# V in transfers of 4 MB and a stream of K and V in bursts, in a decode step of attention beside an MLP

## The chip, the cores and the metric

The kernel runs on one core of one Trainium2 chip. The metric is device microseconds of one execution. A timed run has no profiler; beside it stands one profiled execution, whose own time and span are given below.

## What is computed

One decode step (one new position) for a batch of 8, width D = 576. Two branches read the same x and are mixed by a gate:

```python
g = sigmoid((x * gate_w).sum(-1))            # one gate a batch
q = (x @ wq)                                  # 32 heads of 128
k, v = the last W = 2048 of 8192 positions    # 16 heads of K and V, each for two heads of q
o = softmax(q k^T / sqrt(128)) v              # for each batch and head
a = o @ wo                                    # 4096 -> 576
b = gelu(layernorm(x) @ w1 + b1) @ w2 + b2    # 576 -> 4608 -> 576
out = g * a + (1 - g) * b
```

All data are bfloat16. K and V within the window are 67 MB each, the weights some 20 MB; the rest is small.

## The kernel before, in words

**A plan, then five lists.** The kernel first describes all its work as operations with an engine, a cost and dependences (`_Plan`, lines 40 to 203). `schedule` walks through them in planned time, with a DMA rate of 428 GB/s and the costs given by hand, and so fixes the order of instructions on each engine; `emit` writes that order out, with semaphore waits where they are needed. At run time each engine goes through its own list in order. SyncE (SP) issues all large loads, in the order in which they are created, because each names the one before in `after`; a load that waits for its buffer holds back all loads behind it. ScalarE's queue issues the few small ones at the beginning (x, gate_w, b1).

**Buffers.** One arena in SBUF holds everything. Its largest part is `RAW`: nine slots of 2 MB (128 partitions of 16 KB). At the beginning wq lies in slots 0 to 2 and w1 in slots 3 to 5; slots 6 to 8 are empty. Hence line 642: slots 0 to 2 are free after the q projection (`o_qp`, lines 529 to 538, matmuls recorded at lines 411 and 413), slots 3 to 5 after the hidden layer's matmuls (`o_hp`, lines 560 to 571, the same two lines with other shapes).

**The beginning.** From x (line 451, sixteen rows: the batch twice) VectorE builds a spread and transposed x (lines 466 to 476), then the sums and the normalisation (477 to 491), gate and masks; then it transposes the projected q out of PSUM (line 541). ScalarE and TensorE turn that into query blocks (543 to 557). The hidden layer's five groups of matmuls come behind `o_qT` and behind the loads of w1 (line 570). The gate enters the second branch at line 494 (`dg`, for b2) and in `hs_fn` (598 to 601, for the hidden values).

**The stream.** Sixteen heads of K and V are taken in eight groups `g` of two heads; a group has four units `q` of K and four of V: head `2g + q // 2`, four batches, 2 MB. In a slot, a partition holds 64 positions of one batch in a row.
- `k_unit` (707 to 758) loads a K unit, VectorE transposes it in two halves (line 726, a STREAM_TRANSPOSE each), TensorE multiplies the query block with it (helpers at lines 405 and 420) into four PSUM banks that collect a whole group. After the fourth unit `softmax` follows: maximum on VectorE (672), exponentials on ScalarE (681), transposition of the weights (684). A K slot is free after its two transposes.
- `v_unit` (760 to 770) loads a V unit. When all four of a group have landed, `v_batch` multiplies (line 784, 64 matmuls a group), picks and folds the result (798 to 818) and scales it (`om_fn`, 822). V slots are free after the group's matmuls. The last group is done in two halves (`FULL`).
- `sums` and `rows` (687, 696) give the softmax's denominators for two groups; `wo_chunk` (832) loads a quarter of wo, forms rows by head and multiplies them into the result; its rows `oP` are cut at line 850.
- `bias` and `m2_chunk` (858, 866) load b2 and the four chunks of w2 at the end, the last in four pieces.

**The order of the loads** is `stream` (624 to 639): five K units ahead, then K and V in turn, a wo chunk after every eighth V unit, b2 and w2 at the end. `take_slot` (662) gives any of these the slot that an estimate (`slot_est`) says is free first. K, V, wo and w2 share all nine slots.

Of the kernel before, what the change touches and what calls it, by code (L numbers as in the profile page):

```python
# [8 lines left out]
ACTF = mybir.ActivationFunctionType  # L9
# [203 lines left out]
def build_kernel(nc, A_x, A_k_cache, A_v_cache, A_wq, A_wo, B_x, B_w1, B_b1, B_w2, B_b2, gate_w, out):  # L213
# [25 lines left out]
    with ExitStack() as es:  # L239
# [142 lines left out]
        def col(i, parts=128):  # L382
            return cols[0:parts, i:i + 1]
# [64 lines left out]
        o_qz = add("pool", lambda e: e.memset(view("qbd"), 0.0), name="qbd0", cost=1.0)  # L448


        d_x = dma("act", lambda e: e.dma_start(x_sb, bass.AP(x2.tensor, offset=x2.offset, ap=[[0, 2], [D, 8], [1, D]])), "x", 16 * D * 2, name="d_x")
        d_gw, d_gw1 = [dma("act", (lambda r0=r0, r1=r1: lambda e: e.dma_start(gw_sb[r0:r1, :], gate_w.partition_broadcast(r1 - r0)))(), "gw", (r1 - r0) * D * 2, name="d_gw%d" % r0, after=[d_x])
                       for r0, r1 in ((0, 6), (6, 8))]
        d_b1 = dma("act", lambda e: e.dma_start(b1c[0:FC, :], B_b1.rearrange("(c f) -> c f", c=FC)), "b", F * 2, deps=[o_pad], name="d_b1", after=[d_gw1])
        dx, dgw, db = [d_x], [d_gw, d_gw1], [d_b1]
        d_wqr = dma("sp", lambda e: e.dma_start(wq_r, A_wq[512:576, :].rearrange("k (s c) -> (k s) c", s=2)), "wq", 64 * 8192, name="d_wqr")
        d_wqm = dma("sp", lambda e: e.dma_start(wq_m.rearrange("p t c -> p (t c)"), A_wq[0:512, :].rearrange("(p t) c -> p (t c)", t=4)), "wq", 512 * 8192, name="d_wqm", after=[d_wqr])
        dwq = [d_wqm, d_wqr]
# [32 lines left out]
                                                               b1c[:, 32 * FJ * q:32 * FJ * (q + 1)].rearrange("p (i j) -> p j i", j=FJ)))(), deps=db, name="b1T%d" % q, cost=0.4, after=o_yT[-1:]) for q in range(4)]  # L491
        o_g = add("dve", lambda e: e.tensor_scalar(out=col(C_G), in0=col(C_T), scalar1=0.5, scalar2=0.5, op0=ALU.mult, op1=ALU.add), deps=[o_t] + o_tq, name="g", cost=0.12)
        o_omg = add("dve", lambda e: e.tensor_scalar(out=col(C_OMG), in0=col(C_T), scalar1=-0.5, scalar2=0.5, op0=ALU.mult, op1=ALU.add), deps=[o_t] + o_tq, name="omg", cost=0.12)
        o_dgb = add("dve", lambda e: e.tensor_scalar(out=dg, in0=idf8, scalar1=col(C_OMG, 8), scalar2=None, op0=ALU.mult), deps=[o_omg, o_idf], name="dgb", cost=0.12)

        def gb_fn(e):
            src = bass.AP(arena_f, offset=foffs("cols") + C_G, ap=[[AST // 2, 128], [1, 2], [0, 32]])
# [98 lines left out]
        o_hf = add("dve", lambda e: e.scalar_tensor_tensor(out=v1_sb, in0=v2_sb, scalar=1.0, in1=uh_sb, op0=ALU.add, op1=ALU.mult), deps=[o_th, o_uh], name="hf", cost=0.4)  # L596

        def hs_fn(e):
            in1 = bass.AP(arena_f, offset=foffs("gb") + 32, ap=[[AST // 2, 128], [0, FT], [1, 8]])
            return e.tensor_tensor(out=hT, in0=v1_sb.rearrange("p (t b) -> p t b", b=8), in1=in1, op=ALU.mult)  # L600
        o_hT = add("dve", hs_fn, deps=[o_hf, o_gb], name="hT", cost=0.4)


# [17 lines left out]


        NUQ = 4 * NG
        stream = [("K", i) for i in range(5)]
        ki, vi = 5, 0
        while ki < NUQ or vi < NUQ:
            if ki < NUQ:
                stream.append(("K", ki))
                ki += 1
            if vi % 8 == 3:  # L630
                stream.append(("R", vi // 4))
            if ki >= 6:
                stream.append(("V", vi))
                if (vi + 1) % (NUQ // (Hq // WO_CH)) == 0:
                    stream.append(("W", vi // (NUQ // (Hq // WO_CH))))
                vi += 1
                if vi % 8 == 3:
                    stream.append(("S", vi // 4))
        stream += [("B", 0)] + [("M", i) for i in range(FC)]

        last_dma = [d_w1r]
# [9 lines left out]
        sel_done, oP_ev, rc_last, sum_pe = [], [], [], {}  # L651

        def src_of(cache, g, q):
            hkv, b0 = 2 * g + q // 2, 4 * (q % 2)
            return cache[b0:b0 + 4, hkv, S0:Sk, :].rearrange("a (x r) d -> x a (r d)", x=32)

        FULL = 7
        slot_est = [18.0 + s for s in range(3)] + [38.0 + s for s in range(3)] + [s - 9.0 for s in range(3)]
        landed = [22.0]
        UT, WT = 4 * W * Dh * 2 / P.DMA_BW, WO_CH * 128 * D * 2 / P.DMA_BW  # L660

        def take_slot(took, hold):
            landed[0] += took
            s = min(range(NSLOT), key=lambda s: slot_est[s])
            assert slot_free[s] is not None
            slot_est[s] = landed[0] + hold
            return s

        def softmax(g):
# [36 lines left out]

        def k_unit(i):
            g, q = divmod(i, 4)
            s = take_slot(UT, 8.0)
            d = dma("sp", lambda e: e.dma_start(slot(s), src_of(A_k_cache, g, q)), "s%d" % s, 4 * W * Dh * 2, deps=slot_free[s], name="dk%d" % i, after=last_dma[-1:])  # L710
            last_dma.append(d)
            ub = q
            qrs = []
            if q == 0:
                def qr_fn(e):
                    dst = bass.AP(arena, offset=aoffs("qbd"), ap=[[AST, 128], [128, 16], [32, 4], [1, 8]])
                    in0 = bass.AP(arena, offset=aoffs("q4") + 128 * g, ap=[[AST, 128], [8, 16], [0, 4], [1, 8]])
                    in1 = bass.AP(arena_f, offset=foffs("mq"), ap=[[AST // 2, 128], [0, 16], [1, 4], [0, 8]])
                    return e.tensor_tensor(out=dst, in0=in0, in1=in1, op=ALU.mult)  # L719
                qrs.append(add("pool", qr_fn, deps=[o_q4, o_qz, o_mq, qk_unit.get(i - 1)], name="qr%d" % g, cost=0.8))  # L720
            trs = []
            for h in range(2):
                n = 2 * i + h
                kb = n % 2
                deps = [d] + ([qk_half[n - 2]] if n >= 2 else [o_ssq])
                tr = add("dve", (lambda h=h, kb=kb: lambda e: e.transpose(bass.AP(arena_f, offset=foffs("KT") + kb * 2048, ap=[[AST // 2, 128], [1, 2048]]),  # L726
                                                                         bass.AP(arena_f, offset=foffs("RAW") + s * (SE // 2) + 32 * h, ap=[[AST // 2, 128], [64, 64], [1, 32]])))(),
                         deps=deps, name="tr%d_%d" % (i, h), cost=2.3, after=tr_hist[-1:])
                tr_hist.append(tr)
                trs.append(tr)  # L730

                first = q == 0 and h == 0

                def qk_fn(e, h=h, kb=kb, first=first):
                    mm = None
                    if first:
                        mm_row(e, maskL, [ps[:, rc, :] for rc in range(2)], [maskR] * 2, True, False)
                        late_wait()
                        for rc in range(2, 4):
                            held_mm(e, ps[:, rc, :], maskL, maskR, True, False)  # L740
# [12 lines left out]
                qk = add("pe", qk_fn, deps=deps, late=late, name="qk%d_%d" % (i, h), cost=1.95 + (0.9 if first else 0), after=qk_half[-1:])  # L753
                qk_half.append(qk)
            qk_unit[i] = qk
            slot_free[s] = trs
            if q == 3:
                softmax(g)

        def v_unit(i):  # L760
            g, q = divmod(i, 4)
            full = g < FULL
            s = take_slot(UT, (3 - q if full else q == 0) * 2 * UT + (10.0 if full else 5.0))
            d = dma("sp", lambda e: e.dma_start(slot(s), src_of(A_v_cache, g, q)), "s%d" % s, 4 * W * Dh * 2, deps=slot_free[s], name="dv%d" % i, after=last_dma[-1:])
            last_dma.append(d)
            v_wait.append((q, s, d))
            slot_free[s] = None
            if q == 3 or not full and q >= 1:
                v_batch(g, list(v_wait))
                v_wait.clear()  # L770
# [59 lines left out]
                oT_done[it] = om  # L830

        def wo_chunk(i):
            s = take_slot(WT, 14.0)
            h0 = WO_CH * i
            dst = slot(s)[:, 0:WO_CH * D]
            d = dma("sp", lambda e: e.dma_start(dst, A_wo[128 * h0:128 * (h0 + WO_CH), :].rearrange("(p t) c -> p (t c)", t=WO_CH)),
# [4 lines left out]
            def rows_fn(e):  # L841
                mm = None
                for h in range(WO_CH):
                    mm = e.matmul(ps[:, bk, 64:64 + 8 * WO_CH], wide[:, 112 - 16 * h:240 - 16 * h], oX[:, i % 2, h, :], start=(h == 0), stop=(h == WO_CH - 1), skip_group_check=True)
                    if h == 0:
# [1 line left out]
                return mm  # L847
            its = range(h0 // 2, (h0 + WO_CH) // 2)
            sel_done.append(add("pe", rows_fn, deps=[oT_done[it] for it in its] + [o_wide, rc_last[-1]] + oP_ev[-1:], late=[[d]], name="orow%d" % i, cost=0.6))
            oP_ev.append(add("act", lambda e: e.activation(out=oP[:, i % 2, :], in_=ps[:, bk, 64:64 + 8 * WO_CH], func=ACTF.Copy),  # L850
                             deps=[sel_done[-1]] + ([proj_ops[i - 2]] if i >= 2 else []), name="oPev%d" % i, cost=0.25, prio=3))
            mms = [(oP[:, i % 2, 8 * t:8 * t + 8], dst[:, t * D:(t + 1) * D]) for t in range(WO_CH)]
            proj_ops[i] = AccGroup("proj%d" % i, mms, [oP_ev[-1], d], cost=0.25 * WO_CH).op
# [10 lines left out]
            o_m2.append(AccGroup("m2_b", [(ob[:, 0:8], b2_sb), (ob[:, 8:16], b2_sb)], ds + [o_obl, o_obh], cost=0.6).op)  # L864

        def m2_chunk(ci):
            s = take_slot(FCW * D * 2 / P.DMA_BW, 6.0)
            dst = slot(s)[:, 0:FJ * D]
            src = B_w2[FCW * ci:FCW * ci + FCW, :].rearrange("(p j) n -> p (j n)", j=FJ)
            cuts = [0, 4, 7, 8, 9] if ci == FC - 1 else [0, FJ]  # L870
# [94 lines left out]
```

## Time and profile before

| What | Value |
|---|---|
| timed runs | median 367.14 us (366.82 to 367.57, 3 runs) |
| the profiled execution, whole | 368.24 us |
| its span, first to last instruction | 366.5 us |
| bytes by DMA | 154.50 MB, mean 422 GB/s |
| TensorE / VectorE busy | 229.9 / 229.5 us (63% each) |
| ScalarE / GpSimd busy | 23.4 / 23.1 us |
| granted TensorE clock, mean | 0.823 |

The page shows one execution. Shares are of the span; a line such as L726 is line 726 of the kernel. A helper's line (405, 411, 413, 420, 616) stands for all who call it. The rows of slices cut the span into 40 equal parts of 9.2 us. "PEld" is TensorE's loading of weights. Times in the span begin at its first instruction.

### The profile page before, as it was taken

Reading aid. Unit: us, or ns where it says so; the run is one execution under the profiler, and the core shown is the slowest. Engines: PE = TensorE matmul, PEld = TensorE weight load, DVE = VectorE, ACT = ScalarE, POOL = GpSimd, SP = SyncE. Lnnn points to the kernel's source line nnn. Section 1 sums busy time; section 2 is a strip of 40 time slices with the busy share of each in tenths; the row PEclk is TensorE's granted clock in tenths of the full one; section 3 lists DMA queues with packets and bytes.
Section 4 is the critical chain, followed back from the end, with each engine's and each line's share of the span. In section 5 each row is a group of like instructions: output and inputs, shape, how many; then the busy total and the mean of one; then the engine's idle time right before and its main releaser. Section 6 shows DMA issues by size and latency. Waiting matters only on the chain.

```text
span 366.5 us, 2720 instructions
## 1 busy us (share of the span) xinstructions
PE 229.9 (63%) x1356; PEld 42.4 (12%) x892; DVE 229.5 (63%) x256; ACT 23.4 (6%) x36; POOL 23.1 (6%) x38
## 2 busy tenths in 40 slices
PE   0319883973956768753965396554965395574674
PEld 0000000000200011100200022000300021002232
DVE  1994899787854586447964655459744765456210
ACT  1001002002000020002000200002000200002000
POOL 8001001001000100001000100000000100000100
PEclk9977997897886669866888889887986689768659
DMA  8999999999999999999999999999999999999994
GB/s 343 429 412 438 426 427 433 431 433 431 431 426 431 427 437 429 431 431 429 431 429 429 427 437 431 427 431 433 429 427 433 432 431 431 431 429 429 424 428 186
DMA packets 11462, 154.50 MB, mean 422 GB/s; under 512 B 1294, under 2 KB 1590, under 8 KB 2106
## 3 DMA queue, kind: packets, MB, share of 16 engines
q1 hardware_dynamic: 11392, 154.29, 98.6%
q8 instruction: 9, 0.15, 0.1%
q10 hardware_dynamic: 58, 0.05, 0.0%
q14 instruction: 3, 0.02, 0.0%
HBM read 154.32 MB, written 0.01 MB: 421 GB/s over the span
## 4 chain that ended last, share of the span: by engine, by line
DMA 47%; DVE 25%; PE 23%; ACT 2%; issue 2%; SPq 1%; DVEq 0%
DMA arena<-in_A_k_cache_dram 40%; PE ps L405 11%; DVE arena L726 10%; DMA arena<-in_B_w_dram 5%; PE ps L420 4%; DVE arena L672 4%; PE ps L784 4%; DVE arena L684 2%; ACT arena L681 2%; DMA arena<-in_A_x_dram 2%; PE ps L413 2%; DVE arena L679 1%; DVE arena L471 1%; PE ps L411 1%; DVE arena L675 1%
## 5 line engine op out<-in xcount | busy, mean ns | idle before, releaser
L726 DVE STREAM_TRANSPOSE arena<-arena 128x2048 f32<-128x2048 f32 x64 | 145.2, 2294 | 72.0 <-DMA arena<-in_A_k_cache_dram 68.9
L405 PE MATMUL ps<-arena 128*128 128x512 bf16 x408 | 141.5, 463 | 0.0
L420 PE MATMUL ps<-arena 128*128 128x512 bf16 x136 | 64.6, 475 | 94.7 <-DVE arena L726 54.1
L420 PEld LDWEIGHTS ps<-arena 128*128 128x128 bf16 x136 | 15.4, 113 | 226.4 <-DVE arena L726 101.4
L784 PE MATMUL ps<-arena 128*32 128x512 bf16 x512 | 33.2, 404 | 2.7 <-DMA arena<-in_A_v_cache_dram 2.7
L672 DVE TENSOR_REDUCE arena<-ps 128x1 f32<-128x2048 f32 x8 | 18.3, 2287 | 25.1 <-PE ps L405 25.1
L681 ACT ACTIVATE arena<-ps,arena 128x2048 bf16<-128x2048 f32 x8 | 15.7, 1967 | 183.4 <-DVE arena L679 183.4
L684 DVE STREAM_TRANSPOSE arena<-arena 128x2048 bf16<-128x2048 bf16 x8 | 18.2, 2275 | 2.1 <-ACT arena L681 2.1
L719 POOL TENSOR_TENSOR arena<-arena 128x512 bf16<-128x512 bf16 x8 | 8.3, 1038 | 170.0 <-PE ps L405 156.6
L411 PE MATMUL ps<-arena 128*32 128x512 bf16 (+2 forms) x40 | 7.3, 708 | 15.4 <-DMA arena<-in_A_wq_dram 15.4
L784 PEld LDWEIGHTS ps<-arena 128*32 128x32 bf16 x512 | 12.6, 100 | 26.7 <-issue 13.0
L827 POOL TENSOR_TENSOR arena<-arena 128x256 bf16<-128x256 f32 (+1 forms) x9 | 6.0, 666 | 153.2 <-ACT arena L818 153.2
L616 PE MATMUL ps<-arena 128*8 128x288 bf16 (+1 forms) x140 | 11.6, 315 | 3.6 <-DMA arena<-in_B_w_dram 2.3
L413 PE MATMUL ps<-arena 128*32 128x384 bf16 (+2 forms) x56 | 9.9, 760 | 0.0
L801 DVE COPY_PREDICATED arena<-arena,ps 128x128 f32<-128x128 int32 x30 | 9.0, 300 | 1.0
L800 DVE COPY arena<-ps 128x128 f32<-128x128 f32 x10 | 2.7, 275 | 10.1 <-PE ps L784 10.0
L809 PE MATMUL ps<-arena 128*128 128x32 f32 (+2 forms) x20 | 4.4, 298 | 6.8 <-DVE arena L801 6.8
L891 DVE CAST arena<-ps 8x288 bf16<-8x288 f32 x1 | 0.4, 446 | 12.4 <-PE ps L616 12.4
L818 ACT ACTIVATE arena<-ps 128x32 f32<-128x32 f32 (+1 forms) x9 | 2.0, 221 | 96.1 <-PE ps L809 96.1
L471 DVE TENSOR_SCALAR arena<-arena 16x64 bf16<-16x64 bf16 (+1 forms) x6 | 4.0, 798 | 5.1 <-DMA arena<-in_A_x_dram 5.0
L616 PEld LDWEIGHTS ps<-arena 128*8 128x8 bf16 (+1 forms) x140 | 6.0, 92 | 8.0 <-DMA arena<-in_B_w_dram 3.7
L549 PE MATMUL ps<-arena 128*128 128x256 bf16 x4 | 1.1, 405 | 7.7 <-ACT arena L543 7.7
(78 smaller groups left out, 63.6 us busy)
## 6 DMA issues: line engine op xcount, KB each, us to landing
arena<-in_A_k_cache_dram SPq DMA_DIRECT2D x32, 2048.0 KB, 30.0
arena<-in_A_v_cache_dram SPq DMA_DIRECT2D x32, 2048.0 KB, 29.5
arena<-in_B_w_dram SPq DMA_DIRECT2D x1, 4608.0 KB, 24.3
arena<-in_A_wo_dram SPq DMA_DIRECT2D x4, 1152.0 KB, 29.6
arena<-in_A_wq_dram SPq DMA_DIRECT2D x1, 4096.0 KB, 14.1
arena<-in_B_w_dram SPq DMA_DIRECT2D x3, 1296.0 KB, 17.4
arena<-in_B_w_dram SPq DMA_DIRECT2D x2, 576.0 KB, 21.3
arena<-in_A_wq_dram SPq DMA_DIRECT2D x1, 512.0 KB, 3.4
```

The costliest lines, as they stand in the source:

```text
L405: return e.add_instruction(mybir.InstMatmult(name=nc.get_next_instruction_name(), ins=[e.lower_ap(rhs), e.lower_ap(lhsT)], outs=[e.lower_a ...
L411: mm = e.matmul(outs[0], lhsT, rhss[0], start=start, stop=stop, skip_group_check=True, tile_position=pos)
L413: mm = e.add_instruction(mybir.InstMatmult(name=nc.get_next_instruction_name(), ins=[e.lower_ap(r), e.lower_ap(lhsT)], outs=[e.lower_ap(o) ...
L420: mm = e.matmul(outs[0], lhsT, rhss[0], start=start, stop=stop)
L616: ins = e.matmul(ps[32 * j:32 * j + 8, BK_ACC, 0:JN], lhsT, rhs[:, JN * j:JN * j + JN], start=first and i == 0, stop=True, skip_group_chec ...
L672: mx = add("dve", lambda e: e.tensor_reduce(out=k(MX), in_=ps[:, 0:4, :].rearrange("p a n -> p (a n)"), axis=AXL.X, op=ALU.max), deps=[qk_ ...
L681: ex = add("act", lambda e: e.activation(out=Pm, in_=ps[:, 0:4, :].rearrange("p a n -> p (a n)"), func=ACTF.Exp, bias=k(NB), scale=SCALE, ...
L684: pt_done[g] = add("dve", lambda e: e.transpose(bass.AP(arena, offset=aoffs("PT") + (g % 2) * 2048, ap=[[AST, 128], [8, 64], [512, 4], [1, ...
L719: return e.tensor_tensor(out=dst, in0=in0, in1=in1, op=ALU.mult)
L726: tr = add("dve", (lambda h=h, kb=kb: lambda e: e.transpose(bass.AP(arena_f, offset=foffs("KT") + kb * 2048, ap=[[AST // 2, 128], [1, 2048]]),
L784: mm = e.matmul(ps[32 * t:32 * t + 32, bank, :], PT[:, g % 2, q, 32 * r4:32 * r4 + 32], slot(s)[:, 512 * r4:512 * r4 + 512], start=j < 4, ...
L801: return e.copy_predicated(buf, bass.AP(arena_i, offset=foffs("m4") + r, ap=[[AST // 2, 128], [0, 128]]), src)
```

## The change

Three things go together.

**One V transfer for all eight batches.** A V head's two units are now loaded by one DMA of 4 MB into two neighbouring slots: a partition takes 64 positions of two batches that follow each other, 32 KB, and so the first slot holds the even batches, the second the odd ones. To match, K units take every second batch instead of four in a row. The batch order inside the kernel thereby is 0, 2, 4, 6, 1, 3, 5, 7: x is loaded in that order by two DMAs of eight rows each, and the places where the order meets the outer one (the b2 rows, the hidden values, `oP`) write with a changed pattern. The last group's V is still loaded in units of 2 MB.

**Bursts.** Eight K units come first; then, for each group, its V, (after every second one) a wo chunk, and the K of the group after the next.

**Slots.** V of the first seven groups always uses slots 0 to 3. K, wo and the last V go round slots 6, 7, 8, 4, 5. The four w2 chunks use slots 0 to 3.

```diff
-        d_x = dma("act", lambda e: e.dma_start(x_sb, bass.AP(x2.tensor, offset=x2.offset, ap=[[0, 2], [D, 8], [1, D]])), "x", 16 * D * 2, name="d_x")
+        d_x0, d_x = [dma("act", (lambda s: lambda e: e.dma_start(x_sb[8 * s:8 * s + 8, :], bass.AP(x2.tensor, offset=x2.offset, ap=[[D, 2], [2 * D, 4], [1, D]])))(s), "x", 8 * D * 2, name="d_x%d" % s)
+                     for s in range(2)]
...
-        dx, dgw, db = [d_x], [d_gw, d_gw1], [d_b1]
+        dx, dgw, db = [d_x0, d_x], [d_gw, d_gw1], [d_b1]
...
-        stream = [("K", i) for i in range(5)]
-        ki, vi = 5, 0
-        while ki < NUQ or vi < NUQ:
...
+        stream = [("K", i) for i in range(8)]
+        for g in range(NG):
+            if g % 2 == 0:
+                stream += [("S", g), ("R", g)]
+            stream += [("V", 4 * g + q) for q in range(4)]
+            if g % 2:
+                stream.append(("W", g // 2))
+            if g + 2 < NG:
+                stream += [("K", 4 * (g + 2) + q) for q in range(4)]
         stream += [("B", 0)] + [("M", i) for i in range(FC)]
...
-            hkv, b0 = 2 * g + q // 2, 4 * (q % 2)
-            return cache[b0:b0 + 4, hkv, S0:Sk, :].rearrange("a (x r) d -> x a (r d)", x=32)
+            return cache[q % 2:B:2, 2 * g + q // 2, S0:Sk, :].rearrange("a (x r) d -> x a (r d)", x=32)
...
-        def take_slot(took, hold):
-            landed[0] += took
-            s = min(range(NSLOT), key=lambda s: slot_est[s])
...
+        ring = [6, 7, 8, 4, 5]
+
+        def take_slot():
+            s = ring.pop(0)
+            ring.append(s)
             return s
...
-            s = take_slot(UT, (3 - q if full else q == 0) * 2 * UT + (10.0 if full else 5.0))
-            d = dma("sp", lambda e: e.dma_start(slot(s), src_of(A_v_cache, g, q)), "s%d" % s, 4 * W * Dh * 2, deps=slot_free[s], name="dv%d" % i, after=last_dma[-1:])
-            last_dma.append(d)
+            s = q if full else take_slot()
+            if not full:
+                d = dma("sp", lambda e: e.dma_start(slot(s), src_of(A_v_cache, g, q)), "s%d" % s, 4 * W * Dh * 2, deps=slot_free[s], name="dv%d" % i, after=last_dma[-1:])
+                last_dma.append(d)
+            elif q % 2:
+                src = A_v_cache[0:B, 2 * g + q // 2, S0:Sk, :].rearrange("a (x r) d -> x a (r d)", x=32)
+                d = dma("sp", lambda e: e.dma_start(RAW[:, (q - 1) * SE:(q + 1) * SE], src), "s%d" % (q - 1), 8 * W * Dh * 2, deps=slot_free[q - 1] + slot_free[q], name="dv%d" % i, after=last_dma[-1:])
+                last_dma.append(d)
+            else:
+                d = None
...
         def m2_chunk(ci):
-            s = take_slot(FCW * D * 2 / P.DMA_BW, 6.0)
+            s = ci
```

Left out: the four patterns that put the batches back in order (`dg`, `hT`, `oP` and their sources), each one instruction as before.

More of the change, by code (lines that the diff above doesn't have):

```diff
@@ L493, in build_kernel @@
         o_omg = add("dve", lambda e: e.tensor_scalar(out=col(C_OMG), in0=col(C_T), scalar1=-0.5, scalar2=0.5, op0=ALU.mult, op1=ALU.add), deps=[o_t] + o_tq, name="omg", cost=0.12)
-        o_dgb = add("dve", lambda e: e.tensor_scalar(out=dg, in0=idf8, scalar1=col(C_OMG, 8), scalar2=None, op0=ALU.mult), deps=[o_omg, o_idf], name="dgb", cost=0.12)
+        o_dgb = add("dve", lambda e: e.tensor_scalar(out=dg.rearrange("p (b s) -> p s b", s=2), in0=idf8.rearrange("p (s b) -> p s b", s=2), scalar1=col(C_OMG, 8), scalar2=None, op0=ALU.mult), deps=[o_omg, o_idf], name="dgb", cost=0.12)
         def gb_fn(e):
@@ L598, in hs_fn @@
         def hs_fn(e):
-            in1 = bass.AP(arena_f, offset=foffs("gb") + 32, ap=[[AST // 2, 128], [0, FT], [1, 8]])
-            return e.tensor_tensor(out=hT, in0=v1_sb.rearrange("p (t b) -> p t b", b=8), in1=in1, op=ALU.mult)
+            in1 = bass.AP(arena_f, offset=foffs("gb") + 32, ap=[[AST // 2, 128], [0, FT], [4, 2], [1, 4]])
+            return e.tensor_tensor(out=hT.rearrange("p t (b s) -> p t s b", s=2), in0=v1_sb.rearrange("p (t s b) -> p t s b", s=2, b=4), in1=in1, op=ALU.mult)
         o_hT = add("dve", hs_fn, deps=[o_hf, o_gb], name="hT", cost=0.4)
@@ L623, in build_kernel @@
         NUQ = 4 * NG
-        stream = [("K", i) for i in range(5)]
-        ki, vi = 5, 0
-        while ki < NUQ or vi < NUQ:
[L627 to L638, printed above, removed]
+        stream = [("K", i) for i in range(8)]
[7 more added lines that the diff above has]
+                stream += [("K", 4 * (g + 2) + q) for q in range(4)]
         stream += [("B", 0)] + [("M", i) for i in range(FC)]
@@ L653, in src_of @@
         def src_of(cache, g, q):
-            hkv, b0 = 2 * g + q // 2, 4 * (q % 2)
-            return cache[b0:b0 + 4, hkv, S0:Sk, :].rearrange("a (x r) d -> x a (r d)", x=32)
+            return cache[q % 2:B:2, 2 * g + q // 2, S0:Sk, :].rearrange("a (x r) d -> x a (r d)", x=32)
         FULL = 7
-        slot_est = [18.0 + s for s in range(3)] + [38.0 + s for s in range(3)] + [s - 9.0 for s in range(3)]
-        landed = [22.0]
-        UT, WT = 4 * W * Dh * 2 / P.DMA_BW, WO_CH * 128 * D * 2 / P.DMA_BW
-        def take_slot(took, hold):
-            landed[0] += took
-            s = min(range(NSLOT), key=lambda s: slot_est[s])
-            assert slot_free[s] is not None
-            slot_est[s] = landed[0] + hold
+        ring = [6, 7, 8, 4, 5]
+        def take_slot():
+            s = ring.pop(0)
+            ring.append(s)
             return s
@@ L708, in k_unit @@
             g, q = divmod(i, 4)
-            s = take_slot(UT, 8.0)
+            s = take_slot()
             d = dma("sp", lambda e: e.dma_start(slot(s), src_of(A_k_cache, g, q)), "s%d" % s, 4 * W * Dh * 2, deps=slot_free[s], name="dk%d" % i, after=last_dma[-1:])
@@ L762, in v_unit @@
             full = g < FULL
-            s = take_slot(UT, (3 - q if full else q == 0) * 2 * UT + (10.0 if full else 5.0))
-            d = dma("sp", lambda e: e.dma_start(slot(s), src_of(A_v_cache, g, q)), "s%d" % s, 4 * W * Dh * 2, deps=slot_free[s], name="dv%d" % i, after=last_dma[-1:])
-            last_dma.append(d)
+            s = q if full else take_slot()
[8 more added lines that the diff above has]
+                d = None
             v_wait.append((q, s, d))
-            slot_free[s] = None
             if q == 3 or not full and q >= 1:
@@ L832, in wo_chunk @@
         def wo_chunk(i):
-            s = take_slot(WT, 14.0)
+            s = take_slot()
             h0 = WO_CH * i
@@ L849, in wo_chunk @@
             sel_done.append(add("pe", rows_fn, deps=[oT_done[it] for it in its] + [o_wide, rc_last[-1]] + oP_ev[-1:], late=[[d]], name="orow%d" % i, cost=0.6))
-            oP_ev.append(add("act", lambda e: e.activation(out=oP[:, i % 2, :], in_=ps[:, bk, 64:64 + 8 * WO_CH], func=ACTF.Copy),
+            oP_ev.append(add("act", lambda e: e.activation(out=oP[:, i % 2, :].rearrange("p (t b s) -> p t s b", b=4, s=2), in_=ps[:, bk, 64:64 + 8 * WO_CH].rearrange("p (t s b) -> p t s b", s=2, b=4), func=ACTF.Copy),
                              deps=[sel_done[-1]] + ([proj_ops[i - 2]] if i >= 2 else []), name="oPev%d" % i, cost=0.25, prio=3))
```

## The prediction

> **What bounds the kernel now.** I read the head of the profile's page first, then the DMA queues, then stretches of the span.
>
> ```profile
> span 366.5 us, 2720 instructions
> ...
> GB/s 343 429 412 438 426 427 433 431 433 431 431 426 431 427 437 429 431 431 429 431 429 429 427 437 431 427 431 433 429 427 433 432 431 431 431 429 429 424 428 186
> ...
> q1 hardware_dynamic: 11392, 154.29, 98.6%
> ...
> DMA 47%; DVE 25%; PE 23%; ACT 2%; issue 2%; SPq 1%; DVEq 0%
> ...
> L726 DVE STREAM_TRANSPOSE arena<-arena 128x2048 f32<-128x2048 f32 x64 | 145.2, 2294 | 72.0 <-DMA arena<-in_A_k_cache_dram 68.9
> ...
> L784 PE MATMUL ps<-arena 128*32 128x512 bf16 x512 | 33.2, 404 | 2.7 <-DMA arena<-in_A_v_cache_dram 2.7
> ```
>
> The chain gives DMA only 47%, but it follows one dependence after another. The better view is SP's queue q1: its packets keep the 16 DMA engines busy for 98.6% of the span, and no slice between the first and the last falls below 412 GB/s. A stretch of 40 us, the busiest for VectorE, shows the same from another side (the columns are the stretch, its length, the busy time of TensorE, its weight loads, VectorE, ScalarE and GpSimd, then clock, DMA share and GB/s):
>
> ```profile
> 46.00:86.00 40.00, 27.95 (x108) 2.60 (x26) 34.33 (x25) 2.06 (x2) 2.08 (x2) 0.91 1.01 430
> ```
>
> The queue is never empty, and at 430 GB/s the 154.29 MB alone take 358.8 us of the 366.5. VectorE, the busiest engine beside it, has 34.3 us of work in these 40. So the change can win only by a higher rate or by the few microseconds at the two ends, and it loses whatever time it lets the queue run empty.
>
> The end has a little air in it:
>
> ```profile
> 360.00:361.00 1.00, 0.36 (x6) 0.28 (x8) 0.00 (x0) 0.00 (x0) 0.00 (x0) 1.00 0.89 347
> 361.00:362.00 1.00, 0.91 (x16) 0.46 (x10) 0.00 (x0) 0.00 (x0) 0.00 (x0) 1.00 0.56 203
> 362.00:363.00 1.00, 0.66 (x8) 0.27 (x8) 0.00 (x0) 0.00 (x0) 0.00 (x0) 1.00 0.08 30
> 363.00:364.00 1.00, 0.70 (x10) 0.30 (x10) 0.00 (x0) 0.00 (x0) 0.00 (x0) 1.00 0.09 28
> ```
>
> The shares add up to 1.62 engine-microseconds per engine after 360: the mean DMA engine is done at about 361.6, and the last at about 363.9. From 362 on, 0.08 of 16 is little more than one engine. One engine lags the mean by some 2.3 us and all but it are done by about 362.3. A hole that most engines see costs nothing until it is larger than their 1.6 us of lead.
>
> **The change part by part.** *The bytes* stay: 28 V blocks of 2 MB become 14 transfers of 4 MB, K stays at 2 MB. I price the 14 saved transfer boundaries at 0. With 2 MB transfers, the stretch already runs at 430 GB/s and a DMA share of 1.01, so a boundary hides no time that a share could show. Bounds: 438 GB/s is the best slice of the page; V's 58.7 MB at 438 in place of 430 would be 58.7/430 - 58.7/438 = 2.5 us faster. At 412, the worst slice, it would be 6.0 us slower.
>
> The Trainium skill, page "DMA: Bandwidth & Descriptors", section "Anatomy of one DMA", gives a DMA about 2 us of fixed cost; by that, 14 fewer would save 28 us. The trace does not agree for transfers queued back to back (share 1.01), so that sum is not used.
>
> *The stream in its steady part.* A K block of 2.097 MB takes 4.88 us at 430 GB/s, a burst of four 19.5 us, a V group as long. Two transposes of a K block take VectorE 2 x 2.29 = 4.59 us, so it keeps pace with a burst; the softmax falls into the V half. With five slots in turn, the fifth block after a K block needs that block transposed: the wait falls on a block of the burst before, which is read some 20 us earlier. V's next 4 MB needs the 64 matmuls of the group before; 512 take 33.2 us, so 64 take 4.2, twice that at half clock. Against 8 us stand four K blocks, 19.5 us, already in the queue. Cost 0, margin about 11 us; SP waits there, with the next K blocks behind it, and that delays nothing until the margin is gone. The weights of the output projection pass through the K ring once in two groups and need their slot back 40 us later: 0.
>
> *The end* keeps its order (V of the last head pair in single blocks, output weights, bias, four chunks of B_w2). The chunks get V's four slots, which are free earlier than now; the queue is full there in both: 0. The regrouped batch rows (gate, hidden, oP) change patterns of instructions that exist already: 0, at most tenths of a microsecond off the path.
>
> *The beginning* is where I find a price. The fourth K block now gets slot 4, which held w1 and is free only after the hidden layer's matmuls (line 413). Before, the fourth to sixth K blocks took slots that the query weights had left:
>
> ```profile
> 0.79 0.39 SPq L456 DMA_DIRECT2D arena<-in_A_wq_dram  x1
> ...
> 2.77 18.45 SPq L710 DMA_DIRECT2D arena<-in_A_k_cache_dram  x6
> 37.10 0.53 SPq L764 DMA_DIRECT2D arena<-in_A_v_cache_dram  x1
> 37.85 0.54 SPq L710 DMA_DIRECT2D arena<-in_A_k_cache_dram  x1
> ```
>
> Six blocks were issued by 21.2. The row at 37.85 is the first use of a w1 slot, and SP's wait before it is the end of line 413. In the changed order that is K block 3, and only three blocks (0 to 2) cover the time until then. How long do they last?
>
> ```profile
> 0.00:40.10 40.10, 16.96 (x111) 2.09 (x47) 26.02 (x56) 2.82 (x4) 9.81 (x22) 0.87 0.96 406
> ```
> ```profile
> L710 SPq DMA_DIRECT2D arena<-in_A_k_cache_dram x2: 615/887/1159, 3.5 to 4.7; - x2
> ...
> DMA to landing us min/median/max: 33.9/35.7/37.6
> ```
> ```profile
> 0.00:1.80 1.80, 0.00 (x0) 0.00 (x0) 0.00 (x0) 0.00 (x0) 1.20 (x5) 1.00 0.00 0
> 1.80:2.10 0.30, 0.00 (x0) 0.00 (x0) 0.00 (x0) 0.00 (x0) 0.30 (x2) 1.00 1.32 259
> ```
>
> wq, w1 and three blocks are 4.72 + 5.31 + 6.29 = 16.32 MB, with x 16.35; 406 GB/s x 40.1 us = 16.28 MB, so the mean engine is through with block 2 at 40.2. The next two rows are those of K issues 1 and 2 (at 3.5 and 4.7; shortest, median and longest time to landing): block 2 lands at 4.7 + 37.6 = 42.3, less some 0.3 from data to landing 42.0 for the slowest engine. The first issue, at 0.79, moved its first byte at 1.8: 1.0 us. Block 3 would move from 37.85 + 1.0 = 38.9, 1.3 us before the mean engine runs dry and 3.1 before the slowest does. So the hole is (delay of line 413) - 1.3 us for the mean engine.
>
> Line 413 will be later, since it hangs on x:
>
> ```profile
> 0.79 7.14 DMA arena<-in_A_x_dram
> 8.03 2.07 DVE arena L471 x3
> ...
> 25.45 1.17 DVE arena L541
> ...
> 27.08 1.14 PE ps L549 x4
> ...
> 37.09 0.74 PE ps L413 x6
> ```
>
> From x's landing at 7.93 VectorE works without a pause to the transpose of q (line 541), then ScalarE, the selection matmuls, the hidden layer. A delay d of x goes through in full. Its small DMAs share the engines with wq rows of 32 KB, each 32768 B / (430/16 GB/s) = 1.22 us. These are the packets of ACT's queue in the windows 0 to 4.3, 4.3 to 6.2 and 6.2 to 8.03:
>
> ```profile
> q10 hardware_dynamic: 14, 0.02, 1.3%
> ```
> ```profile
> q10 hardware_dynamic: 5, 0.00, 0.7%
> ```
> ```profile
> q10 hardware_dynamic: 8, 0.00, 0.7%
> ```
> ```profile
> 0.79 1.22 ACTq L451 DMA_DIRECT2D arena<-in_A_x_dram  x1
> 2.04 0.66 ACTq L452 DMA_DIRECT2D arena<-in_gate_w_dram  x2
> ```
>
> Fourteen went before the big rows were under way, then about one per 1.22 us and engine: from 4.3 to 7.93 are three turns, the last rows of x and its completion. Now x comes in two DMAs; the second is issued at 2.04 instead of with the first. It misses the quick start, and its eight rows, on few engines as x's three turns suggest, take four turns and one for the completion. Starting at 5.3 to 6.2 (the turn after a wait like that of the first, about 2.9 us from the issue) it lands at 10.5 to 11.4: d = 2.6 to 3.5. Bounds: 0, if both halves fit into the quick start, and 6, two turns more. I take 3.4, for ACT's second issue stood at 2.04 and its packets show only past 4.3. The hole: 3.4 - 1.3 = 2.1 us for the mean engine, 0.3 for the slowest. At the end the others have 1.6 us of lead, so +0.5 us (2.1 - 1.6; the laggard itself gives 0.3).
>
> The Trainium skill, page "DMA: Bandwidth & Descriptors", section "Queues, rings and completion order", has each DMA engine go round-robin between its queues packet by packet; this agrees with the turns of 1.22 us.
>
> **Sum.** Against the profiled execution: 366.5 + 0.5 = 367.0 us of span. That execution took 368.24 in all; the median of the three timed runs is 367.14. I add the +0.5 to the median: **367.6 us**. About 0.2% (0.73 us) is what a measurement of this kernel can tell from no change.
>
> **The rivals.** *Cover holds* (x's halves both make the quick start, d under 1.3): no hole, 367.1. For it: 14 small packets passed by 4.3. Against it: the second issue comes 1.25 us later.
>
> *A longer hole, slower.* Place: before K block 3. From d = 3.7 on (mean hole 2.4) it passes 0.73 us at the end and then costs one for one. With one or two turns more, d = 4.6 to 5.9, the mean hole is 3.3 to 4.6: +1.7 to +3.0; I take +2.0, 369.1. A slow-clock stretch over line 413 would act alike.
>
> *A better rate.* V at 435 GB/s in place of 430: 58.7/430 - 58.7/435 = 1.6 us, 365.5. For it: slices of 437 and 438. Against it: whole stretches of 40 us stay at 430.
>
> *V's slots starve the queue.* With PV's end 11 us later than I reckon, each of seven groups loses what goes beyond; 1 us each is +7, 374.
>
> *Strided batches.* K blocks now take every second batch, 67 MB apart in place of 33.5 (16 heads x 8192 x 128 x 2 B a batch). If that brought K's 67.1 MB to the page's worst mid slice, 412: 67.1/412 - 67.1/430 = 6.8 us, 373.9. Nothing in the trace speaks for it, since steps of 33.5 MB run at 430. The Trainium skill, same page, has a row on HBM row pitch at large powers of two, where doubling a pitch of 2 MiB took the rate from 164 to 103 GB/s; no run here shows such a loss.
>
> **How the numbers follow.** Forecast, with a hole of up to 2.4 us (367.1 to 367.9): 0.42. Cover holds: 0.12. Longer hole: 0.24. Better rate: 0.11. Starved: 0.07. Strided: 0.04. Faster by over 0.2% is the better rate, 0.11. Slower is the longer hole, the starved and the strided case, 0.35, and 0.04 from the forecast's upper edge: 0.39. The rest, 0.50, is within 0.2%. The range goes from 366.4 (half of the better rate) to 369.4 (the longer hole but for its last part).
>
> **What would show it.** Right: the first instruction of line 471 at 10.5 to 11.5 in place of 8.03; SP's fourth K issue waiting for line 413 and standing near 41.3; GB/s in the stretch 40 to 44 well under 430, and from there 430 without a dip to the end. Wrong: no dip there (cover), a dip at each V group (starved), a level other than 430 in all K bursts (strided) or all V bursts (better rate). All would be wrong if another instruction order on VectorE held the K ring.

## The result and the profile after

| What | Before | After |
|---|---|---|
| timed runs, median | 367.03 us (6 runs) | 370.59 us (370.44 to 371.41, 6 runs) |
| ratio | | 1.0098 [1.0085, 1.0111] |
| profiled execution, whole / span | 368.24 / 366.5 us | 371.41 / 369.5 us |

The change costs 3.6 us. The page of the changed kernel, its head, slices, SP's queue and the chain:

```profile
span 369.5 us, 2710 instructions
...
GB/s 339 431 419 431 266 430 429 429 426 410 424 426 427 428 435 431 436 431 429 426 433 432 427 436 424 438 427 429 435 429 433 429 433 427 431 433 431 425 427 241
...
q1 hardware_dynamic: 11168, 154.29, 98.1%
...
DMA 64%; DVE 15%; PE 15%; SPq 1%; issue 1%; ACT 1%; ACTq 0%
```

The same bytes, and the same 430 GB/s in nearly every slice; the fifth slice (37 to 46 us) has 266. The chain's larger DMA share (it now runs from one V transfer to the next) says nothing about the loss: it counts what followed what, in a queue that was full in both kernels. Around the fifth slice, the stretches of two microseconds (the last column is GB/s). Before:

```profile
40.00:42.00 2.00, 2.00 (x11) 0.19 (x2) 1.93 (x4) 0.44 (x1) 0.00 (x0) 1.00 0.96 410
42.00:44.00 2.00, 1.17 (x6) 0.19 (x2) 2.00 (x3) 0.44 (x1) 0.00 (x0) 1.00 1.07 459
44.00:46.00 2.00, 1.41 (x8) 0.10 (x1) 2.00 (x3) 0.00 (x0) 0.00 (x0) 1.00 1.02 430
```

After, and then what SP issued and what it waited for:

```profile
40.00:42.00 2.00, 2.00 (x21) 0.21 (x5) 0.00 (x0) 0.00 (x0) 0.00 (x0) 1.00 0.10 41
42.00:44.00 2.00, 2.00 (x10) 0.20 (x3) 1.87 (x3) 0.00 (x0) 0.00 (x0) 1.00 0.41 131
44.00:46.00 2.00, 2.00 (x11) 0.19 (x2) 1.93 (x4) 0.45 (x1) 0.00 (x0) 1.00 0.93 393
```
```profile
42.05 1.83 SPq L700 DMA_DIRECT2D arena<-in_A_k_cache_dram  x3
```
```profile
SPq L700 <- PE ps L413: 36.8, 1, 36.8
```

From 40.75 to 43.25 the queue moves nothing. SP's fourth K issue (line 700 is the K load's line in the changed kernel) waited 36.8 us for the hidden layer's matmuls and came at 42.05, where before such an issue came at 37.85 with six blocks already in the queue. The chain from x to there:

```profile
2.04 10.84 DMA arena<-in_A_x_dram
...
12.91 1.44 DVE arena L472 x3
...
29.69 1.17 DVE arena L542
...
31.31 1.13 PE ps L550 x4
...
41.28 0.75 PE ps L413 x7
```

x is read first at 12.91 in place of 8.03, 4.9 us later. Of that, 4.2 reach VectorE's transpose of q (29.69 against 25.45; the first group of line 472 is shorter here) and the end of line 413.

One number sums it up: the mean rate from 0 to 90 us, and from 90 to 350. Before, then after:

```profile
0.00:90.00 90.00, 49.39 (x236) 5.17 (x78) 70.00 (x95) 7.82 (x10) 11.88 (x24) 0.89 0.99 419
90.00:350.00 260.00, 170.62 (x1018) 32.18 (x712) 157.86 (x157) 14.81 (x23) 10.73 (x13) 0.80 1.01 430
```
```profile
0.00:90.00 90.00, 49.42 (x240) 5.40 (x86) 66.35 (x89) 5.76 (x8) 11.88 (x24) 0.89 0.95 401
90.00:350.00 260.00, 159.85 (x1000) 33.70 (x687) 159.92 (x160) 16.85 (x25) 10.71 (x13) 0.80 1.01 430
```

After 90 us the two means do not differ. Before it, 18 GB/s x 90 us are missing; at 430 GB/s that is 3.8 us of queue time, and 3.6 us is what the runs lost. (Within these 3.8, the hole itself is 3.4, as reckoned below; the rest is a slightly lower rate from 46 on in this one execution.)

### The profile page after: what moved, and what is told of

The parts are those of the page before. It is cut to its first block, busy times and chain, and to the rows that moved or that the text cites. A ratio compares the mean times of both kernels' runs of the same rounds, so it can differ in the third digit from the quotient of the medians.

```text
span 369.5 us, 2710 instructions
## 1 busy us (share of the span) xinstructions
PE 221.6 (60%) x1356; PEld 45.3 (12%) x892; DVE 228.6 (62%) x256; ACT 23.4 (6%) x36; POOL 23.0 (6%) x38
## 4 chain that ended last, share of the span: by engine, by line
DMA 64%; DVE 15%; PE 15%; SPq 1%; issue 1%; ACT 1%; ACTq 0%
DMA arena<-in_A_v_cache_dram 54%; PE ps L780 10%; DVE arena L716 7%; DMA arena<-in_B_w_dram 7%; DMA arena<-in_A_x_dram 3%; PE ps L413 2%; PE ps L405 1%; DVE arena L662 1%; ACT arena L671 1%; SPq L759 1%; DVE arena L472 1%; PE ps L411 1%; DVE arena L491 1%; DVE arena L474 1%; DVE arena L674 1%
## 5 line engine op out<-in xcount | busy, mean ns | idle before, releaser
L716 DVE STREAM_TRANSPOSE arena<-arena 128x2048 f32<-128x2048 f32 x64 | 143.4, 2286 | 25.7 <-DMA arena<-in_A_k_cache_dram 17.2
L405 PE MATMUL ps<-arena 128*128 128x512 bf16 x408 | 119.0, 401 | 0.0
L780 PE MATMUL ps<-arena 128*32 128x512 bf16 x512 | 47.1, 543 | 49.3 <-DMA arena<-in_A_v_cache_dram 49.3
L420 PE MATMUL ps<-arena 128*128 128x512 bf16 x136 | 55.5, 408 | 24.6 <-DVE arena L716 18.7
L420 PEld LDWEIGHTS ps<-arena 128*128 128x128 bf16 x136 | 13.6, 100 | 139.7 <-DVE arena L716 82.0
L780 PEld LDWEIGHTS ps<-arena 128*32 128x32 bf16 x512 | 16.7, 128 | 78.3 <-DMA arena<-in_A_v_cache_dram 54.8
L683 PE MATMUL ps<-arena 128*128 128x64 f32 x8 | 2.8, 448 | 27.5 <-DVE arena L681 27.5
```

The source lines that it names most:

```text
L405: return e.add_instruction(mybir.InstMatmult(name=nc.get_next_instruction_name(), ins=[e.lower_ap(rhs), e.lower_ap(lhsT)], outs=[e.lower_a ...
L420: mm = e.matmul(outs[0], lhsT, rhss[0], start=start, stop=stop)
L780: mm = e.matmul(ps[32 * t:32 * t + 32, bank, :], PT[:, g % 2, q, 32 * r4:32 * r4 + 32], slot(s)[:, 512 * r4:512 * r4 + 512], start=j < 4, ...
```

## The experiments

The theory: x comes late, so line 413 ends late, so slot 4 comes free late, and with three K blocks of cover the queue runs empty; nothing else of the change costs or gains. The rivals: 4 MB transfers or strided batches move more slowly; bursts and fixed slots lose time later; the late x costs by itself. Each of the runs below changes one link.

**e1, x earlier.** The second half of x goes to SP's queue, between the two loads of wq, the first of which is now issued ahead of x (abridged; gate_w's DMAs now follow the first half of x):

```diff
+        d_wqr = dma("sp", ...)
-        d_x0, d_x = [dma("act", ...
+        d_x0, d_x = [dma(("act", "sp")[s], ... after=[d_wqr][:s])
-        d_wqm = dma("sp", ... after=[d_wqr])
+        d_wqm = dma("sp", ... after=[d_x])
```

> The changed kernel, with the second half of x issued on SP's queue, behind the first 512 KB of wq and ahead of its 4 MB, in place of ScalarE's queue. Theory (the late x opens a hole in the queue before K block 3): x lands by 8 us in place of 12.9, the end of line 413 comes back to 38 us or earlier, the stretch 40 to 44 shows 420 GB/s or more, and the time falls to 366.9 to 367.5. Rival (transfers of 4 MB or batches 67 MB apart move at a lower rate): the hole goes in part, but the time stays above 369. Rival (bursts and fixed slots lose time later): the hole goes, time 368 to 370, with dips in the middle.

Measured: 368.98 us, ratio 1.0057 [1.0036, 1.0077]. x is read first at 4.36, line 413 ends at 37.3, and the hole is gone (410 and 459 GB/s from 40 to 44). But the first four microseconds move at 203 GB/s in place of 258 (before) and 264 (after). The next four move at 354 in place of 395 (before), but e2, whose beginning is that of the changed kernel, has 337 there, so this second number proves little. That x now stands in the way of wq in the same queue is the likely reading; no run isolates it. The time is not what the theory said, nor the rate rival. It lies in the range of the rival "bursts and fixed slots lose time later", but the dips in the middle that this rival needs are not there: from 90 us on no stretch of 10 us falls below 421 GB/s, and the mean to 350 is 431. The rates up to 90 us account for 4 GB/s x 90 us, or 0.8 us. The profiled run was the fastest of four and lost 1.1; the median lost 1.8, and what the slower runs lost beyond that is not explained. e8 below mends x without this side effect.

**e2, other slots, x late.** K blocks 3, 4 and 5 go to slots 0, 1, 2 (`head` is used up first, then `ring` goes round):

```diff
         ring = [6, 7, 8, 4, 5]
+        head = [6, 7, 8, 0, 1, 2]
```

> The changed kernel, x as late as in it; only K blocks 3, 4 and 5 go to slots 0, 1, 2, which the query weights leave early, in place of 4, 5, 6. Theory (hole before K block 3, because slot 4 waits for line 413): six blocks are issued by 22 us, no hole although x still lands at 12.9 and line 413 still ends at 42; 366.9 to 367.6. Rival (the late x costs by itself, as VectorE is behind by 4.9 us): 369.5 to 370.6 without a hole. Rival (rate of 4 MB or strided transfers): above 369.

Measured: 372.6 us, ratio 1.0155 [1.0130, 1.0180]: slower still, and the theory's number failed. The hole before block 3 is gone, but a new one opens 25 us later. Stretches of two microseconds, then SP:

```profile
64.00:66.00 2.00, 0.00 (x0) 0.00 (x0) 1.85 (x8) 0.86 (x1) 0.00 (x0) 1.00 0.65 279
66.00:68.00 2.00, 0.75 (x2) 0.10 (x1) 2.00 (x2) 1.19 (x2) 0.00 (x0) 0.52 0.02 8
68.00:70.00 2.00, 2.00 (x6) 0.15 (x1) 1.64 (x1) 0.00 (x0) 0.00 (x0) 0.50 0.68 229
```
```profile
67.47 10.25 SPq L762 DMA_DIRECT2D arena<-in_A_v_cache_dram  x2
```

V's first transfer needs slots 0 and 1, which now hold K blocks 3 and 4, and VectorE, which is late by x and takes the first group's softmax before block 4, frees the second one only at 67.4. The mistake was in the experiment, but it says something: a late x does no harm by itself, it does harm wherever a load asks for what hangs on it.

**e3, two DMAs for x in the kernel before**, eight rows each in the natural order (`ap=[[4 * D, 2], [D, 4], [1, D]]`, rows 0 to 7).

> The kernel before, with x alone loaded by two DMAs of eight rows (in the natural batch order). Theory (a late x costs only where the cover is three blocks): x lands at 12 to 13, line 413 ends near 42, six K blocks are already queued, 366.8 to 367.4. Rival (the late x itself is the price): 370 to 371.

Measured: 366.98 us, ratio 0.9996 [0.9986, 1.0005]. The time is as expected, but not for the reason: x was not late at all. It was read first at 6.56, earlier than with one DMA:

```profile
1.40 5.14 DMA arena<-in_A_x_dram
...
6.56 3.41 DVE arena L472 x3
```

So two DMAs do not make x late; two DMAs in the regrouped row order do. The packets on ScalarE's queue show how. The rows of SP's and ScalarE's small loads are the same in all kernels; what differs is the number of completions. Before, after, and e3:

```profile
q10 hardware_dynamic: 58, 0.05, 0.0%
```
```profile
q10 hardware_dynamic: 60, 0.05, 0.0%
```
```profile
q10 hardware_dynamic: 72, 0.05, 0.1%
```

Of these, 56 are common. One x DMA before leaves 2 completions, the two of the changed kernel 2 + 2, the two of e3 8 + 8: read with the rule below, with rows 0, 2, 4, 6, 1, 3, 5, 7 a DMA uses two engines with four rows each, with rows 0 to 7 it uses eight with one each. The order also sets when the second DMA is issued: at 1.40 in e3, at 2.04 in the changed kernel.

The Trainium skill, page "DMA: Bandwidth & Descriptors", section "Why a DMA increments its semaphore by 16 and not by 1", says that the number of engines is the largest up to 16 that divides the slowest dimension of both access patterns, and that each of them posts one completion. The trace agrees: 2 for a pattern that begins with `[D, 2]`, 8 for eight rows in a run (e3's pattern, written `[4 * D, 2], [D, 4]`, counts as such a run; e8's `[D, 8]` has the same 72 packets).

Few engines alone do not make x late. The one DMA of the kernel before has 2 completions too, and x is read at 8.03; e1 has the regrouped order, one DMA on each of two queues, and reads x at 4.36. Late is the second of two such DMAs behind each other in ScalarE's queue.

**e4, V in units of 2 MB** (the kernel's own line for the last group, used for all groups).

> The changed kernel with V in transfers of 2 MB into the same slots, order and bursts kept. Theory (the size of a transfer costs and gains nothing): the hole stays, 370.3 to 370.9, as the changed kernel. Rival (4 MB transfers lose rate): 367 to 369.5. Rival (4 MB transfers gain what the hole hides): above 371.2.

Measured: 370.73 us, ratio 1.0097 [1.0081, 1.0113], as the changed kernel; 0 to 90 us at 402 GB/s, then 430. The size of V's transfers neither costs nor gains.

**e5, four blocks of cover, x late.** Only K block 3 moves, to slot 2, which V needs in its second transfer:

```diff
-        ring = [6, 7, 8, 4, 5]
+        head, ring = [6, 7, 8, 2], [4, 5, 6, 7, 8]
```

> The changed kernel, x as late as in it; K block 3 goes to slot 2 (left early by the query weights, used by V only in its second transfer), the ring goes on with 4, 5, 6, 7, 8. Four blocks then cover the time to 45, and line 413 ends at 42. Theory (the loss is the empty queue, not the late x): no stretch of 2 us under 400 GB/s between 8 and 360, time 366.8 to 367.5, as before. Rival (VectorE's lag of 4.2 us must be paid somewhere): a hole at another slot, as with slots 0 to 2, 369 or more. Rival (the rest of the change gains once the hole is closed): under 366.3.

Measured: 367.86 us, ratio 1.0017 [1.0008, 1.0026], with x read first at 13.24. Of the 3.6 us, 2.8 come back with one slot's number changed. A rest of 0.7 us stays, so the time is 0.4 us above the theory's range, and two stretches are below its 400 GB/s: from 44 to 48 the queue moves 377 and 369. Why that dip is there, with block 4 issued at 42.4 and the four blocks of cover lasting until about 45 (40.2 and 4.88 more), is open.

**e6, two blocks of cover** (`ring = [6, 7, 4, 5, 8]`).

> The changed kernel with the ring 6, 7, 4, 5, 8: only two K blocks stand before the first that waits for line 413. Theory (an empty queue costs one for one): the hole grows by one block, 4.9 us, and so does the time: 375.0 to 376.0. Rival (part of a hole is given back later, since the engines have lead at the end): 373 to 374.8.

Measured: 375.55 us, ratio 1.0223 [1.0206, 1.0240]. That is 8.4 us over the kernel before, where the changed kernel lost 3.6: 4.9 us more (each against the kernel before on the same chip), for a cover that is one block (4.88 us) shorter. In the same stretch:

```profile
36.00:38.00 2.00, 2.00 (x16) 0.13 (x4) 0.84 (x1) 0.00 (x0) 0.00 (x0) 1.00 0.00 0
38.00:40.00 2.00, 2.00 (x16) 0.13 (x4) 0.00 (x0) 0.00 (x0) 0.00 (x0) 1.00 0.00 0
40.00:42.00 2.00, 2.00 (x20) 0.13 (x4) 0.00 (x0) 0.00 (x0) 0.00 (x0) 1.00 0.00 0
42.00:44.00 2.00, 1.84 (x12) 0.29 (x3) 1.68 (x2) 0.00 (x0) 0.00 (x0) 1.00 0.49 131
```

An empty queue costs one for one; no part is given back.

**e7, the kernel before with late x and strided batches.** K and V units of every second batch, x by the two DMAs of the changed kernel, with its patterns that put the batches back; order, slots and 2 MB transfers as before.

> The kernel before with K and V units of every second batch, x in that order by the two late DMAs, and the patterns that put the batches back; order, slots and 2 MB transfers as before. Theory (a late x costs nothing behind six queued blocks, and the stride costs nothing): x lands near 12.9, line 413 ends near 42, 366.8 to 367.5. Rival (late x by itself, or strided batches, cost): 368.5 to 371.

Measured: 367.10 us, ratio 0.9993 [0.9982, 1.0004], with x read first at 12.99. The first use of a w1 slot is as late as in the changed kernel:

```profile
42.13 0.54 SPq L710 DMA_DIRECT2D arena<-in_A_k_cache_dram  x1
```

Here it is the seventh K block, behind six others, and the stretch from 40 to 44 moves 410 GB/s. So neither the stride nor the late x costs anything by itself.

**e8, the changed kernel with x in natural order** (`ap=[[D, 8], [1, D]]` in both DMAs; queries and caches then belong to different batches, so only its time is read).

> The changed kernel with x's two DMAs reading eight rows in the natural order (queries and caches then belong to different batches; only the time is read). In the kernel before, two such DMAs landed at 6.6. Theory (x is late because of its row order, not because it comes in two DMAs; and that alone makes the loss): x lands by 7, line 413 ends near 38, no hole, 366.8 to 367.5. Rival (the cover of three blocks is too thin even with an early x): a hole of 0.5 us or more, 367.6 to 369. Rival (two DMAs in this kernel are late in any order): 370.5.

Measured: 367.08 us, ratio 0.9996 [0.9987, 1.0005]. x is read first at 6.65, line 413 ends at 37.7, no hole:

```profile
1.40 5.22 DMA arena<-in_A_x_dram
...
6.65 3.33 DVE arena L472 x3
```
```profile
40.00:42.00 2.00, 2.00 (x10) 0.19 (x2) 1.97 (x3) 0.40 (x1) 0.00 (x0) 1.00 0.96 393
42.00:44.00 2.00, 1.17 (x6) 0.19 (x2) 2.00 (x3) 0.44 (x1) 0.00 (x0) 1.00 0.99 426
```

The whole loss is gone with 4 MB transfers, stride, bursts and slots all in place. This decides the question.

**e9 and e10, versions that keep the batch order.** x in the regrouped order by four DMAs of four rows (one row an engine):

```diff
+        d_xs = [dma("act", (lambda s: lambda e: e.dma_start(x_sb[4 * s:4 * s + 4, :], bass.AP(x2.tensor, offset=x2.offset + D * (s % 2), ap=[[2 * D, 4], [1, D]])))(s), "x", 4 * D * 2, name="d_x%d" % s)
+                for s in range(4)]
```

e10 has e5's slots as well.

> The changed kernel, whole, with x in the regrouped batch order by four DMAs of four rows in place of two of eight: the outer dimension of each is then 4 rows apart by two batches, in place of 2. Theory (x was late since its rows stood four deep behind one another on few engines): one row deep, x lands between 7 and 10, line 413 ends at 38 to 40, no hole of a microsecond or more, 366.9 to 367.5. Rival (more DMAs on ScalarE's queue make it later still): x lands at 12 or later and the time stays at 370 or more. Rival (the change gains once the loss is mended): under 366.3.

> The same with K block 3 in slot 2, the ring going on with 4, 5, 6, 7, 8: x early and four blocks of cover. Theory: no hole, 366.9 to 367.4, not faster than the kernel before, since the queue is full in both. Rival (something of the change gains): under 366.3.

Measured: e9 367.62 us, ratio 1.0013 [1.0002, 1.0024]; e10 367.22 us, ratio 0.9998 [0.9989, 1.0006]. x is read first at 10.45 and 10.31, between the two orders and later than the 7 to 10 expected; e9's time is 0.1 us above the theory's range, e10's within it. In e9 K block 3 is issued at 38.93, just when its data are needed; its twelve runs scatter from 367.14 to 368.86, those of e10, with a block more of cover, from 366.94 to 367.62. The stretch from 40 to 42 in e9, then in e10:

```profile
40.00:42.00 2.00, 2.00 (x11) 0.19 (x2) 1.86 (x6) 0.44 (x1) 0.00 (x0) 1.00 0.93 303
```
```profile
40.00:42.00 2.00, 2.00 (x11) 0.23 (x3) 1.86 (x6) 0.44 (x1) 0.00 (x0) 1.00 0.97 410
```

e10 is the change without its loss, and it is as fast as the kernel before, not faster. No run points to a version that beats it.

**All in one table.** "Missing" is (419 - rate from 0 to 90 us) x 90 / 430, from one profiled execution each; "lost" is the median against that of the kernel before on the same chip.

| Kernel | x read at | K blocks of cover | rate 0 to 90 | missing, us | lost, us |
|---|---|---|---|---|---|
| after | 12.91 | 3 | 401 | 3.8 | 3.6 |
| e4 V in 2 MB | 13.0 | 3 | 402 | 3.6 | 3.6 |
| e6 two ahead | 13.15 | 2 | 379 | 8.4 | 8.4 |
| e2 slots 0, 1, 2 | 12.88 | 6, V waits | 396 | 4.8 | 5.4 |
| e5 slot 2 | 13.24 | 4 | 416 | 0.6 | 0.7 |
| e1 x on SP | 4.36 | 3 | 415 | 0.8 | 1.8 |
| e9 x in four | 10.45 | 3 | 416 | 0.6 | 0.4 |
| e8 x natural | 6.65 | 3 | 420 | -0.2 | -0.1 |
| e10 x in four, slot 2 | 10.31 | 4 | 420 | -0.2 | 0.0 |
| e3 before, two x | 6.56 | 6 | 420 | -0.2 | -0.2 |
| e7 before, late x, stride | 12.99 | 6 | 420 | -0.2 | 0.0 |

From 90 to 350 us all eleven move 430 or 431 GB/s.

## Why the prediction was wrong

The place and the mechanism were right, and so was nearly all that was priced at nothing. Two steps failed, the size of x's delay and the lead at the end that was taken off the hole; with a smaller error in the hole itself they put 370.6 above the range.

**The bound** was right: SP's queue sets the time, and a kernel loses what the queue stands empty (e6).

**Transfers of 4 MB, stride, bursts, slots: 0.** Right (e4, e7, e8). The rivals "better rate", "starved" and "strided batches" fall; so does the sum by 2 us a DMA. The Trainium skill, page "DMA: Bandwidth & Descriptors", section "Anatomy of one DMA", has that figure for DMAs issued by GpSimd. Of SP's queued loads, 14 fewer transfers changed nothing (370.73 us with 2 MB, 370.59 with 4 MB).

**The hole before K block 3** was foreseen with its waits: x, VectorE, line 413, slot 4. The relation "hole = delay of line 413 - 1.3 us" gives 4.2 - 1.3 = 2.9 us; the stretches 40 to 46 moved 41, 131 and 393 GB/s where they had moved 410, 459 and 430, so 2 x (1299 - 565) / 430 = 3.4 us were missing. That is half a microsecond more than the relation has. Part of it is the start from the empty queue: block 3, issued at 42.05, moved its first bytes after 43.25, so at least 1.2 us after its issue, where the relation has 1.0, and 44 to 46 is still under 430.

**Failed: the delay of x, "I take 3.4".** It was 4.9. Nor did this delay go through in full: with the shorter first group of line 472, 4.2 reached line 413. The count of turns was right, their start was not. ScalarE's queue in the changed kernel, windows 0 to 4.3, 6.2 to 8.03 and 8.03 to 12.91 (from 4.3 to 6.2 it has no packet at all):

```profile
q10 hardware_dynamic: 10, 0.01, 0.9%
```
```profile
q10 hardware_dynamic: 6, 0.01, 1.0%
```
```profile
q10 hardware_dynamic: 16, 0.01, 0.7%
```

Ten packets, the first half with its completions, got the quick start. The second half, issued at 2.04, showed nothing before 7.1 (the six packets of the second window all lie from 7.1 to 7.5), where the prediction let it start at 5.3 to 6.2. From there to x's first reading at 12.91 there is room for the five turns of some 1.2 us. Why the second half starts so late is open; in e8 its packets lie from 4.7 to 5.1 and from 6.0 to 6.4. The prediction named the cause that made x two-engine work ("on few engines as x's three turns suggest") but took it for a property of x, and did not see that two DMAs in another row order would have been free of it (e3, e8).

**Failed: "A hole that most engines see costs nothing until it is larger than their 1.6 us of lead."** No such lead was there to be used: 8.4 us missing cost 8.4, 3.8 cost 3.6. The tail of 2.3 us came with an execution that took longer than most: 368.24 us, 1.1 above the median of the timed runs, as the prediction itself had written down. The profiled executions of e5 and e9, 368.41 and 368.27 us, also still move data between 363 and 364 (shares 0.11 and 0.10). e10, whose timed runs are as fast as the kernel before, ends like this:

```profile
360.00:361.00 1.00, 0.88 (x17) 0.43 (x14) 0.00 (x0) 0.00 (x0) 0.00 (x0) 1.00 0.96 372
361.00:362.00 1.00, 0.64 (x8) 0.26 (x8) 0.00 (x0) 0.00 (x0) 0.00 (x0) 1.00 0.57 210
362.00:363.00 1.00, 0.89 (x10) 0.35 (x10) 0.00 (x0) 0.00 (x0) 0.00 (x0) 1.00 0.16 50
```

Its mean engine is done at 361.7 (the shares after 360 add up to 1.69), as before, and its last by 363, not 363.9. With 2.1 us of hole charged in full, the prediction's own d would have given 369.2; with the 4.2 us that reached line 413, the relation gives a hole of 2.9 and 370.0, and the hole of 3.4 that the stretches show gives 370.5. Of the missing 3.0 us, 1.6 are this step, 0.8 the delay (4.2 in place of 3.4) and 0.5 the hole's relation.

The rival "a longer hole" had the right direction and the right place; its price, 369.1, carried the same deduction.

Open: why x's second half starts at 7.1, a part of e1's loss, e5's dip at 44 to 48, and a slightly lower rate from 46 to 126 us in the profiled execution of the changed kernel (425 and 426 GB/s in 40 us each, before 430 and 431), which e4 and e6 do not repeat to that extent. That lower rate is worth 0.9 us, about what this execution lay above its median (371.41 against 370.59).

## What to carry to other kernels

In a kernel whose load queue is full from end to end, look for the first moment at which a load waits for a computation, count the bytes that are queued ahead of it, and charge every microsecond beyond them in full. A small load at the very beginning can set that moment, as x did here: try a row order that spreads it over more engines, and have all of it issued before the big rows start. A tail seen in one profiled execution that is slower than the timed median is not air that a change can use.

## What the runs showed of the hardware

- Two DMAs of eight rows of 1152 B, one behind the other on ScalarE's queue and beside the same stream, differed by their row order. With the rows in a run (e3 and e8, 8 + 8 completions), the second was issued at 1.40 us and complete 5.1 to 5.2 us later; with every second row first (2 + 2 completions), it was issued at 2.04 and complete 10.8 us later.
- One DMA of x on SP's queue and one on ScalarE's (e1) arrive soonest of all (read at 4.36), but the stream moves less beside them: 203 GB/s in place of 258 over the first four microseconds.
- A load issued into an empty queue moved its first bytes after 1.2 us or more (K block 3 of the changed kernel, issued at 42.05).
- Transfers of 2 and of 4 MB, with batches 33.5 or 67 MB apart, all move 430 to 431 GB/s once the queue is full.
